# Sequence DFT table built by GpSimd, batch 1's second pc copy by ScalarE, and lower score prices in the order model

## The chip, the cores and the metric

The kernel runs on one core of one Trainium2 chip. The metric is the device time of one execution in microseconds. A profiled execution also has a span, from its first to its last instruction, which is shorter than its device time.

## What is computed

Inputs are q, k and v of 8 batches, 12 heads, 448 positions and 64 channels, and two weights, w1 (768 x 3072) and w2 (3072 x 768). The reference, cut to what matters:

```python
scores = q @ k.transpose(0, 1, 3, 2) / sqrt(64)
attn   = maximum(scores, 0) ** 2 / 448
x      = (attn @ v), heads side by side            # 8 x 448 x 768
mixed  = real(fft(fft(x, axis=1), axis=2))         # over positions, then channels
u      = x + mixed
un     = (u - mean(u)) / sqrt(var(u) + 1e-6)       # over the 768 channels
out    = u + maximum(un @ w1, 0) @ w2
```

The two transforms are done as matrix products with tables of cosines and sines: a channel table (`chan`, and `chan_neg` with the sign of one half turned) and a sequence table (`seq` with cosines and sines, and `nseq`, the sines with the sign turned).

## The kernel before, in words

**Stages of a batch.** Attention works on 21 items a batch (7 for each group of 4 heads). An item is a pair of score products on TensorE (`score`, L939), a Relu of 128 x 896 by ScalarE (`squares`, L952), a square by VectorE (`square`, L969), and then products with v (`value`, L807 and L812), 24 steps in batch 0. Each of the six finished blocks of 128 channels is copied out of PSUM as `xT` (`leave` in `fold`, L656 and L658 for batch 0, L674 for batch 1) and folded by symmetry (L733 for batch 0). The channel transform multiplies the folds by `chan` (L1392 in `first_channels` for batch 0, L1417 in `mix` later). Its result `pp` has two halves of rows. Each is copied from PSUM to `pc` (L1436). Then the sequence transform multiplies `pc` by `seq` and `nseq` (L1014 in `first_tail` for batch 0, L1229 in `mix_rows` for batch 1), u is formed and normalised, and turned for the two big products (L1905 with w1, L1890 or L1892 for its Relu, L1933 with w2 for the first group of 384 rows).

**Start.** GpSimd issues the loads of q, k, v and the weights in one hand-written order (`loading`): the three groups of batch 0, two groups of batch 1's q and k, six half blocks of w1, the rest of batch 1's k, the other half of w1, batch 1's v, then w2 in four quarters, the fourth issued by the second L511 of its pair. Between the first loads it writes index rows (`dft_indices`: four iotas). From these VectorE makes the angles of the tables (`build_dft`): for each piece a product rounded to integer (L328), the fraction (L330) and its absolute value (L332). ScalarE takes sines (L337). The order in `build_dft` is the sequence table first, then the three channel tables; `negative` makes `nseq` from `seq` on VectorE (L374) and `chan_neg` (L378). The first q and k are turned by TensorE against an identity (L608) and copied by VectorE and ScalarE (L615). After batch 0's last Relu, `root_table` (L384) has ScalarE load the table for square roots, which `first_tail` needs.

**Order of the work.** Every engine runs its queue in order. The order is fixed when the program is built, by the class `Streams`: each piece of work is a step of a generator that names its engine, a price in microseconds, the times before which it can't start, and buffers. `Streams` takes again and again the step that can start first by its own clock, and among equals the one of lowest rank. So a price in `need(...)` does not change an instruction's duration on the chip, but changes where it stands in its queue. The prices of TensorE are multiples of `mm(n)`, `n / 2400 + 0.002` us in this stage, of ScalarE `act(n)`, `n / 1200 + 0.17`, from which its clock takes off `OVERLAP`, 0.12. A score step of batch 0 costs `mm(448) + 0.2` (twice `mm` for one item in seven), a value step the same.

**Batch 1's pc.** `mix` copies the first half of `pp` on ScalarE and the second on VectorE. On VectorE's queue stand also the copies of batch 2's q and k into bf16 (L568), which wait for their loads.

Of the kernel before, what the change touches and what calls it, by code (L numbers as in the profile page):

```python
# [10 lines left out]
FP32 = mybir.dt.float32  # L11
# [166 lines left out]
def kernel(  # L178
# [141 lines left out]
    def build_dft():  # L320
# [14 lines left out]
        def sine(dst, y, n, e, sign=1, bias=zero_t):  # L335
            e = yield need("ACT", act(n), [e + LATENCY["DVE"]])
            nc.scalar.activation(dst, y, AF.Sin, bias=bias, scale=sign * 2.0 * math.pi)  # L337
            dft_ready.t = e + LATENCY["ACT"]

        yield need("DVE", 1.1, [indices_ready])  # L340
        nc.vector.tensor_scalar(row[:, 0:2], row[:, 0:2], 1.0 / S, None, op0=ALU.mult)
        nc.vector.tensor_scalar(row[:, 4:7], row[:, 4:7], 1.0 / D, None, op0=ALU.mult)

        f = work.tile([128, 4 * KH], FP32, name="dfty", tag="uA", bufs=1)
        g = work.tile([128, 4 * KH], FP32, name="dfty", tag="uB", bufs=1)
        for i in range(2):
            e = yield from turns(f[:, i * SX:(i + 1) * SX], g[:, i * SX:(i + 1) * SX], col[:, 0:SX], row[:, i:i + 1], SX, i)
        yield from sine(seq[:, 0, :, :].rearrange("p a s -> p (a s)"), g[:, :2 * SX], 2 * SX, e, -1, halfpi)
        yield from sine(seq[:, 1, :, :].rearrange("p a s -> p (a s)"), f[:, :2 * SX], 2 * SX, e)
        seq_ready.t = dft_ready.t  # L350

        def channel_table(m):
            y = early_hid if m == 2 else work.tile([128, 4 * KH], FP32, name="dfty", tag=("u1A", "u1B")[m], bufs=1)
            e = yield from turns(y[:, 2 * KH:4 * KH], y[:, 0:2 * KH], col2, row[:, 4 + m:5 + m], 2 * KH, m % 2)
            yield from sine(chan[m][:, 0, :], y[:, 0:2 * KH], 2 * KH, e, -1, halfpi)
            yield from sine(chan[m][:, 1, :], y[:, 2 * KH:4 * KH], 2 * KH, e)
            chan_made[m].t = dft_ready.t

        yield from channel_table(0)

        def others():

            for m in (1, 2):
                yield from channel_table(m)
            dft_all.t = dft_ready.t

        sch.add(others(), (0, 0.15))

    chan_made, dft_all = [Cell() for _ in range(3)], Cell()

    def negative():

        e = yield need("DVE", 0.35, [seq_ready])
        nc.vector.tensor_scalar(nseq, seq[:, 1], -1.0, None, op0=ALU.mult)  # L374
        nseq_ready.t = e + LATENCY["DVE"]
# [5 lines left out]
    def root_table():  # L381

        yield need("ACT", 1.5, [dft_all, last_relu])
        nc.scalar.activation(drow[:, 7:8], zero_t, AF.Sqrt, bias=eps_t)  # L384
# [56 lines left out]
    def load_group(i, which=(0, 1, 2), parts=(0, 1)):  # L441
# [3 lines left out]
        for x, src in enumerate((q, k, v)):  # L445
# [19 lines left out]
            if i == 0 and x == 1:  # L465
                e = yield need("POOL", 0.95)
# [50 lines left out]
    def loading():  # L517
# [5 lines left out]
        yield from load_w1(0)  # L523
        yield from load_group(NG, (1,), (1,))
# [876 lines left out]
    def mix(b):  # L1401
# [782 lines left out]
```

## Time and profile before

| | us |
|---|---|
| median of 3 runs | 570.84 (569.85 to 572.52) |
| the profiled execution | 572.27 |
| its span | 570.5 |
| busy: TensorE / VectorE / ScalarE / GpSimd | 557.1 / 443.0 / 315.5 / 195.7 |
| TensorE busy in 0 to 10 and 10 to 20 us | 8.09, 8.22 |

The granted TensorE clock is 1.00 throughout. In lines of a timeline the columns are start, busy time, engine, line, operation, output and inputs with their shapes, and count; in brackets stands how long the engine had been idle and what ended that. In a line of waits stand the waiting line, what it waited for, the microseconds in total, how often, and the longest. Consecutive instructions of an engine overlap a little, so the busy time of one can be longer than its distance to the next.

### The profile page before, as it was taken

The numbers are of one execution on the slowest core, as the hardware profiler recorded it, in microseconds if no ns is written. First come the engines' busy times: TensorE is split into PE (matmuls) and PEld (weight loads), VectorE is DVE, ScalarE is ACT, GpSimd is POOL, SyncE is SP. The second block draws the span as 40 slices with busy tenths as digits, with TensorE's granted clock in tenths as the row PEclk, the third lists the DMA queues.
The fourth block names the chain that finished last, engine by engine and source line by source line (L and its number), as shares of the span: only waits on it lengthen the run. The fifth ranks groups of instructions, "written<-read, shape, count | busy, mean of one in ns | idle before, by whom it ended". The sixth has DMA issues, their size and how long they took to land.

```text
span 570.5 us, 11231 instructions
## 1 busy us (share of the span) xinstructions
PE 557.1 (98%) x4211; PEld 352.0 (62%) x4216; DVE 443.0 (78%) x1028; ACT 315.5 (55%) x526; POOL 195.7 (34%) x279
## 2 busy tenths in 40 slices
PE   7999998999999999999999999999999999999997
PEld 5466555644355555545756766766668688668864
DVE  7977674887788977887998897888899967644762
ACT  5967771576655677676786647718615154005400
POOL 8856223614335233463455536325006000000000
PEclk9999999999999999999999999999999999999999
DMA  9999999979977998899899989947415430332012
GB/s 104 184 210 230 182 216 160 241 129 121 185 94 207 206 152 157 135 205 193 178 128 207 203 132 199 170 122 165 111 56 164 118 98 17 83 108 74 1 55 84
DMA packets 152546, 82.44 MB, mean 145 GB/s; under 512 B 118060, under 2 KB 147756, under 8 KB 152492
## 3 DMA queue, kind: packets, MB, share of 16 engines
q0 software_dynamic: 57056, 33.63, 43.8%
q1 hardware_dynamic: 95436, 48.09, 38.0%
q8 instruction: 33, 0.54, 0.4%
q14 instruction: 21, 0.17, 0.1%
HBM read 62.91 MB, written 26.25 MB: 156 GB/s over the span
## 4 chain that ended last, share of the span: by engine, by line
PE 83%; DMA 9%; DVE 4%; POOL 2%; ACT 1%; issue 1%; SPq 0%; DVEq 0%; POOLq 0%; ACTq 0%
PE psF L1905 23%; PE psF L2045 21%; PE psS L1737 8%; PE psS L939 6%; DMA qn<-in_q_dram 6%; PE psS L2045 5%; PE psF L1960 4%; PE psF L812 4%; PE psF L1933 3%; PE psF L1737 2%; PE psS L1417 2%; DVE sq L969 1%; DMA qk<-in_k_dram 1%; DMA kn<-in_k_dram 1%; PE psF L807 1%
## 5 line engine op out<-in xcount | busy, mean ns | idle before, releaser
L1905 PE MATMUL psF<-unT,w 128*128 128x256 bf16 (+2 forms) x1147 | 165.0, 299 | 1.3 <-DVE hT L1890 0.9
L952 ACT ACTIVATE sq<-psS 128x896 bf16<-128x896 f32 x168 | 144.0, 921 | 32.2 <-PE psS L939 31.8
L1905 PEld LDWEIGHTS <-w 128*128 128x128 bf16 x1152 | 110.8, 98 | 50.9 <-issue 6.7
L969 DVE TENSOR_TENSOR sq<-sq 128x896 bf16<-128x896 bf16 x143 | 89.1, 637 | 9.8 <-ACT sq L952 8.9
L2045 PEld LDWEIGHTS <-hT 128*128 128x128 bf16 x648 | 62.5, 98 | 43.6 <-issue 3.9
L1892 ACT ACTIVATE hT<-psF 128x512 bf16<-128x512 f32 (+2 forms) x118 | 58.0, 507 | 42.6 <-PE psF L1905 41.9
L2045 PE MATMUL psF<-w,hT 128*128 128x384 bf16 x336 | 60.1, 326 | 0.7 <-DVE o L1601 0.6
L1601 DVE TENSOR_TENSOR o<-psF,o 128x384 f32<-128x384 f32 x77 | 42.5, 551 | 23.0 <-PE psF L2045 19.2
L939 PE MATMUL psS<-qkT 64*128 64x448 bf16 (+1 forms) x336 | 51.6, 354 | 2.5 <-DVE qkT L615 1.2
L1752 ACT COPY copies<-psS 128x256 f32<-128x256 f32 x57 | 19.9, 374 | 53.9 <-PE psS L1737 49.0
L1260 POOL TENSOR_TENSOR u<-tp,xn 112x385 f32<-112x385 f32 (+2 forms) x14 | 14.7, 1048 | 80.9 <-DVE tp L1240 61.4
L674 DVE TENSOR_SCALAR xT<-psF 128x224 bf16<-128x224 f32 x62 | 21.2, 384 | 22.6 <-PE psF L812 22.6
L461 POOL DMA_DIRECT2D qn<-in_q_dram x21 | 15.5, 740 | 58.4 <-DVE qkr L568 52.3
L939 PEld LDWEIGHTS <-qkT 64*128 64x128 bf16 (+1 forms) x336 | 13.6, 94 | 34.8 <-issue 29.5
L812 PE MATMUL psF<-sq,vn 128*64 128x448 bf16 x246 | 32.7, 362 | 0.4 <-DVE sq L969 0.4
L1737 PEld LDWEIGHTS <-w 128*128 128x128 bf16 x288 | 28.2, 98 | 4.7 <-issue 1.1
L436 POOL DMA_DIRECT2D kn<-in_k_dram x42 | 25.7, 624 | 12.6 <-PE psF L812 7.0
L1269 DVE BATCH_NORM_STATS2 stats<-u 112x6 f32<-112x384 f32 (+2 forms) x56 | 28.5, 542 | 1.0 <-POOL u L1260 0.8
L436 POOL DMA_DIRECT2D vn<-in_v_dram x42 | 26.0, 633 | 9.4 <-DMA w<-in_moe_w_ch_dram 8.2
L461 POOL DMA_DIRECT2D vn<-in_v_dram x24 | 18.9, 787 | 26.9 <-PE psS L939 26.8
L1288 ACT ACTIVATE un<-u,small 113x768 bf16<-113x768 f32 (+2 forms) x21 | 20.9, 1024 | 10.9 <-DVE small L1275 8.3
L812 PEld LDWEIGHTS <-vn 128*64 128x64 bf16 x288 | 12.7, 108 | 21.5 <-issue 17.0
(236 smaller groups left out, 956.0 us busy)
## 6 DMA issues: line engine op xcount, KB each, us to landing
out_dram<-o SPq DMA_DIRECT2D x56, 192.0 KB, 2.2
qn<-in_q_dram POOLq DMA_DIRECT2D x21, 224.0 KB, 5.0
vn<-in_v_dram POOLq DMA_DIRECT2D x24, 192.0 KB, 5.5
w<-in_moe_w_ch_dram POOLq DMA_DIRECT2D x12, 384.0 KB, 9.1
w<-in_moe_w_ch_dram POOLq DMA_DIRECT2D x4, 1152.0 KB, 26.0
kn<-in_k_dram POOLq DMA_DIRECT2D x21, 192.0 KB, 6.6
utop<-u SPq DMA_DIRECT2D x12, 336.0 KB, 3.6
o<-utop SPq DMA_DIRECT2D x16, 192.0 KB, 4.3
```

What stands on the lines that cost most here:

```text
L436: nc.gpsimd.dma_start(out=t[par * Dh:(par + 1) * Dh, par::2], in_=at)
L461: nc.gpsimd.dma_start(out=to, in_=src[b, hs, 0:rows].rearrange("h (p j) d -> p h (j d)", j=j))
L812: nc.tensor.matmul(av[h * Dh:(h + 1) * Dh, 0:S], lhsT=vn_home[:, at:at + Dh], rhs=sq[:, h, :], start=start, stop=stop, skip_group_check=True)
L939: nc.tensor.matmul(sc[:, h, 0:S].rearrange("k (c q) -> k c q", c=4), lhsT=flat[ps, k0:k0 + KB], rhs=qT[ps, pair], start=True, stop=True)
L952: nc.scalar.activation(r, sc[:, :, 0:S], AF.Relu)
L969: nc.vector.tensor_tensor(r, r, r, op=ALU.mult)
L1269: nc.vector.bn_stats(stats[:n, hf, :], u[:n, hf * (D // 2):(hf + 1) * (D // 2)])
L1601: nc.vector.tensor_tensor(o, pc[:, 0:DH], o, op=ALU.add)
L1737: nc.tensor.matmul(ps[:, 0:N], lhsT=lhs, rhs=rhs[:, m], start=(start and m == 0), stop=(stop and m == 2), skip_group_check=True)
L1892: nc.scalar.activation(hs, ps, AF.Relu)
L1905: nc.tensor.matmul(ph[:, i * N:(i + 1) * N], lhsT=w1_sb[m][hf][:, (jj + i) * 128:(jj + i + 1) * 128], rhs=unT[:, m, 0:N], start=(m == 0), ...
L2045: nc.tensor.matmul(pc[:, 0:DH], lhsT=lhs[i], rhs=rhs[i], start=(start and i == 0), stop=(i == KP - 1), skip_group_check=True)
```

## The change

Three things are changed.

1. The sequence table leaves `build_dft`. A new step `seq_table` in `loading`, after the first half of w1, writes its two index rows and makes its angles on GpSimd, with a rounding by adding and subtracting 1.5 * 2^23. VectorE then takes the absolute value by masking the sign bit, and ScalarE takes three sines, `nseq` among them, after batch 0's last Relu. `root_table` comes after these. In `build_dft` the angles of all three channel tables follow each other, and their sines are steps of their own.
2. Batch 1's second pc copy is made by ScalarE.
3. The prices of batch 0's score and value steps go from `mm(S) + 0.2` to `mm(S) + 0.1`.

```diff
     def dft_indices():
-        nc.gpsimd.iota(drow[:, 0:2], pattern=[[128, 2]], base=0, channel_multiplier=1,
-                       allow_small_or_imprecise_dtypes=True)
         nc.gpsimd.iota(drow[:, 4:7], pattern=[[128, 3]], base=0, channel_multiplier=1,
                        allow_small_or_imprecise_dtypes=True)
-        nc.gpsimd.iota(dcol[:, 0:SX], pattern=[[1, SX]], base=0, channel_multiplier=0,
-                       allow_small_or_imprecise_dtypes=True)
...
-        for i in range(2):
-            e = yield from turns(f[:, i * SX:(i + 1) * SX], g[:, i * SX:(i + 1) * SX], col[:, 0:SX], row[:, i:i + 1], SX, i)
-        yield from sine(seq[:, 0, :, :].rearrange("p a s -> p (a s)"), g[:, :2 * SX], 2 * SX, e, -1, halfpi)
-        yield from sine(seq[:, 1, :, :].rearrange("p a s -> p (a s)"), f[:, :2 * SX], 2 * SX, e)
-        seq_ready.t = dft_ready.t
...
+        for m in range(3):
+            yield from channel_table(m)
+
+    def seq_table():
+
+        f = work.tile([128, 4 * KH], FP32, name="dfty", tag="uA", bufs=1)
+        g = work.tile([128, 4 * KH], FP32, name="dfty", tag="uB", bufs=1)
+        yield need("POOL", 0.55)
+        nc.gpsimd.iota(drow[:, 0:2], pattern=[[128, 2]], base=0, channel_multiplier=1,
+                       allow_small_or_imprecise_dtypes=True)
+        nc.gpsimd.iota(dcol[:, 0:SX], pattern=[[1, SX]], base=0, channel_multiplier=0,
+                       allow_small_or_imprecise_dtypes=True)
+        yield need("POOL", 0.3)
+        nc.gpsimd.tensor_scalar(drow[:, 0:2], drow[:, 0:2], 1.0 / S, None, op0=ALU.mult)
+        for i in range(2):
+            yield need("POOL", 0.45)
+            nc.gpsimd.tensor_scalar(f[:, i * SX:(i + 1) * SX], dcol[:, 0:SX], drow[:, i:i + 1], None, op0=ALU.mult)
+        f, g = f[:, 0:2 * SX], g[:, 0:2 * SX]
+        yield need("POOL", 0.75)
+        nc.gpsimd.tensor_scalar(g, f, ROUND, -ROUND, op0=ALU.add, op1=ALU.add)
+        e = yield need("POOL", 1.1)
+        nc.gpsimd.tensor_tensor(f, f, g, op=ALU.subtract)
+        sch.add(seq_sines(f, g, e + LATENCY["POOL"]), (0, 0.3))
+
+    def seq_sines(f, g, e):
+
+        e = yield need("DVE", 0.4, [e])
+        nc.vector.tensor_scalar(g.bitcast(mybir.dt.int32), f.bitcast(mybir.dt.int32), 0x7FFFFFFF, None,
+                                op0=ALU.bitwise_and)
+        flat = seq.rearrange("p t a s -> p t (a s)")
+        for dst, y, sign, bias in ((flat[:, 0], g, -1, halfpi), (flat[:, 1], f, 1, zero_t),
+                                   (nseq.rearrange("p a s -> p (a s)"), f, -1, zero_t)):
+            e = yield need("ACT", act(2 * SX), [e + LATENCY["DVE"], last_relu])
+            nc.scalar.activation(dst, y, AF.Sin, bias=bias, scale=sign * 2.0 * math.pi)
+        seq_ready.t = nseq_ready.t = dft_ready.t = e + LATENCY["ACT"]
...
     def negative():
 
-        e = yield need("DVE", 0.35, [seq_ready])
-        nc.vector.tensor_scalar(nseq, seq[:, 1], -1.0, None, op0=ALU.mult)
-        nseq_ready.t = e + LATENCY["DVE"]
         for m in range(3):
...
         yield from load_w1(0)
+        yield from seq_table()
         yield from load_group(NG, (1,), (1,))
...
-            e = yield need("PE", (1 + (r == 3)) * mm(S) + 0.2, turned_for(0, i), [BS])
+            e = yield need("PE", (1 + (r == 3)) * mm(S) + 0.1, turned_for(0, i), [BS])
...
-            e = yield need("PE", mm(S) + 0.2, [sqs[i][1], ready[m // 2][2]], [BF] if i == its[0] else [])
+            e = yield need("PE", mm(S) + 0.1, [sqs[i][1], ready[m // 2][2]], [BF] if i == its[0] else [])
...
-            en, copy = ("ACT", nc.scalar.copy) if n0 == 0 else ("DVE", nc.vector.tensor_copy)
+            en, copy = ("ACT", nc.scalar.copy) if n0 == 0 or b == 1 else ("DVE", nc.vector.tensor_copy)
```

More of the change, by code (lines that the diff above doesn't have):

```diff
@@ L337, in sine @@
             nc.scalar.activation(dst, y, AF.Sin, bias=bias, scale=sign * 2.0 * math.pi)
-            dft_ready.t = e + LATENCY["ACT"]
-        yield need("DVE", 1.1, [indices_ready])
-        nc.vector.tensor_scalar(row[:, 0:2], row[:, 0:2], 1.0 / S, None, op0=ALU.mult)
+            dft_made.t = e + LATENCY["ACT"]
+        yield need("DVE", 0.2, [indices_ready])
         nc.vector.tensor_scalar(row[:, 4:7], row[:, 4:7], 1.0 / D, None, op0=ALU.mult)
-        f = work.tile([128, 4 * KH], FP32, name="dfty", tag="uA", bufs=1)
-        g = work.tile([128, 4 * KH], FP32, name="dfty", tag="uB", bufs=1)
-        for i in range(2):
-            e = yield from turns(f[:, i * SX:(i + 1) * SX], g[:, i * SX:(i + 1) * SX], col[:, 0:SX], row[:, i:i + 1], SX, i)
-        yield from sine(seq[:, 0, :, :].rearrange("p a s -> p (a s)"), g[:, :2 * SX], 2 * SX, e, -1, halfpi)
-        yield from sine(seq[:, 1, :, :].rearrange("p a s -> p (a s)"), f[:, :2 * SX], 2 * SX, e)
-        seq_ready.t = dft_ready.t
         def channel_table(m):
@@ L354, in channel_table, with sines @@
             e = yield from turns(y[:, 2 * KH:4 * KH], y[:, 0:2 * KH], col2, row[:, 4 + m:5 + m], 2 * KH, m % 2)
+            sch.add(sines(m, y, e), (0, 0.15))
+        def sines(m, y, e):
             yield from sine(chan[m][:, 0, :], y[:, 0:2 * KH], 2 * KH, e, -1, halfpi)
             yield from sine(chan[m][:, 1, :], y[:, 2 * KH:4 * KH], 2 * KH, e)
[L357 to L365, printed above, removed]
@@ L371, in negative @@
+    ROUND = 1.5 * 2 ** 23
+    chan_made, dft_made = [Cell() for _ in range(3)], Cell()
     def negative():
[L373 to L375 removed]
         for m in range(3):
```

7 lines of the change are left out of this document (3 added, 4 removed).

## The prediction

> **What bounds the kernel now.** I read the page first, then the waits of TensorE, then a table of windows, and only then single instructions.
>
> ```profile
> span 570.5 us, 11231 instructions
> PE 557.1 (98%) x4211; PEld 352.0 (62%) x4216; DVE 443.0 (78%) x1028; ACT 315.5 (55%) x526; POOL 195.7 (34%) x279
> ```
>
> TensorE is busy for 557.1 of 570.5 us. So a gain can only be idle time of TensorE taken away, or TensorE work that starts earlier. The waits from 50 us on, and the windows around the changed places:
>
> ```profile
> PE psS L1229 <- DVE pc L1436: 1.7, 1, 1.7
> PE psF L1905 <- DVE hT L1890: 0.9, 1, 0.9
> ```
>
> ```profile
> 20.00:31.00 11.00, 10.10 (x72) 3.87 (x69) 11.00 (x30) 10.99 (x16) 7.20 (x14) 1.00 1.12 188
> 31.00:36.00 5.00, 5.00 (x46) 3.47 (x46) 2.75 (x10) 2.55 (x5) 1.36 (x3) 1.00 1.18 204
> ```
>
> The columns of the windows are length, then TensorE, its weight loads, VectorE, ScalarE, GpSimd, each with its count, then clock, DMA share and GB/s. The largest wait after 50 us is batch 1's second pc copy, the very one that moves. In batch 0's attention VectorE (11.00 of 11.00) and ScalarE (10.99) are both full. So that stage is bound by these two, and batch 0's tail follows it. The chain of waits agrees; its pieces there are:
>
> ```profile
> 15.95 2.54 ACT sq L952 x3
> ...
> 21.41 2.01 DVE sq L969 x4
> ...
> 32.82 3.09 PE psS L1392 x30
> ```
>
> **Part one: the second pc copy of batch 1.**
>
> ```profile
> 90.98 1.04 ACT L1436 CAST pc<-psS 128x772 bf16<-128x772 f32 x1 [4.48 <-PE psS L1417]
> ...
> 91.78 2.11 PE L1933 MATMUL psF<-w,hT 128*128 128x384 bf16 x12
> ...
> 93.73 0.33 PE L1229 MATMUL psS<-pc,seqm 128*128 128x385 bf16 x1
> 94.37 0.43 DVE L568 COPY qkr<-qn 112x1024 bf16<-112x1024 bf16 x1 [5.37 <-DMA qn<-in_q_dram]
> ...
> 94.72 1.01 DVE L1436 CAST pc<-psS 97x772 bf16<-97x772 f32 x1
> ...
> 95.78 1.32 PE L1229 MATMUL psS<-pc,seqm 97*128 97x385 bf16 x7 [1.73 <-DVE pc L1436]
> ...
> 96.47 0.49 ACT L1237 ACTIVATE qs<-psS 128x385 f32<-128x385 f32 x1 [4.46 <-PE psS L1229]
> ...
> 96.94 1.30 PE L1933 MATMUL psF<-w,hT 128*128 128x384 bf16 x7
> ```
>
> The copy needs 1.01 us but stands behind L568, which waits 5.37 us for batch 2's q. The reader sees TensorE issue one row matmul at 93.73 and the next at 95.78. Seven rows take 96.94 - 95.78 = 1.16 us, 0.17 each, so the second was due at 93.90: 1.88 us are lost. After the change ScalarE does both copies, the first to about 92.0, the second at the first's 1.04 us to about 93.1. It has nothing else until 96.47. Both are ready before 93.73, so I take the whole **1.9 us** (bounds 0, if another wait stands there, and 1.9). Next late after that is nothing that the rows name: L1933 goes on at once.
>
> **Part two: the sequence table leaves the start.**
>
> ```profile
> 4.41 0.36 DVE L328 TENSOR_SCALAR dftr<-early,drow 128x240 int32<-128x240 f32 x1
> ...
> 6.60 0.41 DVE L332 SCALAR_TENSOR_TENSOR dfty<-dfty 128x240 f32<-128x240 f32 x1
> ...
> 7.04 1.28 ACT L337 ACTIVATE seqm<-dfty,few 128x480 bf16<-128x480 f32 x2 [5.03 <-DVE dfty L332]
> ...
> 8.80 0.28 DVE L374 TENSOR_SCALAR nseq<-seqm 128x480 bf16<-128x480 bf16 x1
> ...
> 9.98 0.65 DVE L615 COPY qkT<-psF 128x960 bf16<-128x960 bf16 x1
> ...
> 11.14 1.12 ACT L337 ACTIVATE chan<-dfty,few 128x386 bf16<-128x386 f32 x2 [0.25 <-DVE dfty L332]
> ...
> 12.17 0.90 ACT L952 ACTIVATE sq<-psS 128x896 bf16<-128x896 f32 x1
> ...
> 12.97 1.11 ACT L337 ACTIVATE chan<-early,few 128x386 bf16<-128x386 f32 x2
> ```
>
> VectorE loses six operations between 4.41 and 7.01 and nseq at 8.80, 2.9 us; ScalarE loses two sines, 1.28. The three channel tables then follow at once, so all their sines should be over near 10.4 instead of 14.0 (12.97 and 1.11 of busy time). The first score does not gain: its q and k copy (9.98) now stands behind all nine table operations and three negations. But once the relus start, at about 12 as before, the pair of sines at 12.97 is no longer between them: 1.0 us of ScalarE, and 0.26 us of idle time at 15.95 (quoted below) goes too. I take **1.3 us** (bounds 0, if group 1's k keeps the pace, and 2.1, if both later pairs of sines and the idle time count).
>
> **Part three: the same table on GpSimd.** What its load queue waits for between 20 and 36 us, and the rows for the prices:
>
> ```profile
> POOL w L500 <- DMA w<-in_moe_w_ch_dram: 5.2, 4, 1.4
> ...
> POOL kn L436 <- DMA w<-in_moe_w_ch_dram: 2.3, 2, 1.3
> ```
>
> ```profile
> 24.19 1.27 POOL L436 DMA_DIRECT2D kn<-in_k_dram  x2
> 40.53 0.99 POOL L1087 TENSOR_SCALAR un<-u,small 128x768 bf16<-128x768 f32 x1
> ...
> 101.65 1.04 POOL L1260 TENSOR_TENSOR u<-tp,xn 128x385 f32<-128x385 f32 x1
> ...
> 105.84 0.55 DVE L1262 TENSOR_TENSOR u<-tp,xn 112x383 f32<-112x383 f32 x1
> ...
> 169.52 1.14 POOL L1262 TENSOR_TENSOR u<-qs,xn 113x383 f32<-113x383 f32 x1
> 169.89 1.19 DVE L1262 TENSOR_TENSOR u<-tp,xn 113x383 f32<-113x383 f32 x1
> ```
>
> By elements, 240 columns of a tensor_scalar cost 0.31 us, 480 cost 0.62, the 480-column subtraction 1.30: four readers of SBUF, 2.54 us, and with the two iotas and the tiny scaling about 3.4. These stand ahead of the kn issue at 24.19. In this stretch GpSimd waits six times, 7.5 us in all, until an earlier weight block has landed, so I count the delay as **0**: the halves of k lie behind six blocks of weights whenever they are issued. If that cover fell away, batch 1's k would come up to 3.4 us later. At the start the loads behind the two iotas that leave are issued a little earlier; that is 0 as well, since the first score waits for VectorE's copy. Nothing that SP issues is moved.
>
> What is not hidden is VectorE. At 169.89 a VectorE operation with two SBUF inputs took 1.19 us against 0.55 at 105.84, and it ended just 0.42 us after the GpSimd operation beside it had ended: it waited for it. Batch 0's squares are such operations, and VectorE is full there. [...]
>
> [...]
>
> Added on VectorE is one absolute value of 480 columns, about **-0.5** from the 0.36 us of L328's 240. It is also a new wait: behind it in VectorE's queue stand the next squares and folds, and behind those TensorE's values. The plan allots GpSimd 3.6 us; the rows give 3.4, but four readers that each wait for a running square (2.01 / 4 = 0.5 us) make 5.4. So VectorE may stand for 0 to 2.0 us; I take **0**, since a low rank lets squares go first.
>
> **Part four: three sines at the end, and the order.**
>
> ```profile
> 15.95 0.92 ACT L952 ACTIVATE sq<-psS 128x896 bf16<-128x896 f32 x1 [0.26 <-PE psS L939]
> ...
> 31.27 1.28 ACT L384 ACT_TABLE_LOAD   x1
> ...
> 33.66 0.46 DVE L733 TENSOR_TENSOR fold<-xT 128x225 bf16<-128x225 bf16 x2
> ...
> 35.28 1.06 ACT L1436 CAST pc<-psS 128x386 bf16<-128x386 f32 x2 [2.42 <-PE psS L1392]
> ```
>
> Three sines at 0.64 us make 1.9, inside the 2.42 us that ScalarE waits for L1392: **0**, with 0.5 us of cover; without that cover they cost up to 1.9.
>
> The order model now charges TensorE 0.1 us less for each of 45 scores and values. By its old prices (mm, act and OVERLAP in the code) TensorE had 18.1 us of them against 16.7 us of relus and was full, so L1392 came behind the last values: 30 of its 36 instructions run from 32.82 on, 3.09 us to 35.91. By the new ones TensorE has 13.6 us, and the first half fits between scores. Only the last channel block of both halves, 8 instructions of 3.09 / 30 = 0.10 us, must follow the last fold, which ends at 33.66 + 0.46 = 34.12. That makes 34.9 at the earliest: a bound of 1.0 us, the other is 0. I take **0.9 us**.
>
> Front: 1.3 - 1.5 - 0.5 + 0.9 = **+0.2 us** earlier. What passes on of it is limited by a transfer:
>
> ```profile
> L511 POOL DMA_DIRECT2D w<-in_moe_w_ch_dram x4: 826/841/856, 53.1 to 59.6; - x4
> ...
> DMA to landing us min/median/max: 17.8/26.0/31.9
> ```
>
> The last quarter of w2 is issued at 59.6 and lands 31.9 us later, at 91.5; the first matmul that needs it (the fourth chain of L1933) runs at 91.78. So only 0.3 us of any front gain gets past, unless the loads move too; they were backlogged, by the 26.0 us that the median took. A front loss has no such limit. Sum: 0.2 + 1.9 = **2.1 us**. The profiled execution took 572.27 us (span 570.5), which becomes 570.2; it lay 1.43 above the median of the runs, so by the median 570.84 becomes **568.7**.
>
> **The rivals.** [...] (2) *The moved copy gains nothing*, because the plan, which now counts the two copies in a row, puts another late instruction ahead of the rows. Only 0.2 is left: 570.6. Against it: no other producer is late at 93.73. (3) *VectorE waits for GpSimd*, slower than before. [...] It decides from the point where the front loses more than 1.9. For it: VectorE has no idle time in 20 to 31. Against it: the rank.
>
> **How the numbers follow.** The forecast, 568.7, has 0.45, its own range 567.5 to 570.0 from the spread of the runs; (1) 0.28, (2) 0.10, (3) 0.17. The range 566.5 to 572.6 leaves out the better edge of (1) and the worse half of (3). A measurement tells 0.5% from no change, 2.85 us here: below 568.0 lie all of (1) and 0.10 of the forecast, 0.38; above 573.7 lies the far part of (3), where the later order suffers as well, 0.11; between them 0.51.
>
> **What would show it.** Right: no wait of L1229 for pc; channel sines over before the first relu; VectorE squares beside GpSimd readers of 0.9 us or more; few L1392 after the last value; the L1933 chain near 91.5. Wrong: an idle VectorE before the absolute value, ScalarE late with batch 0's pc, or the weights of w2 landing earlier with the work; and a new order in later batches whose waits are over 1 us.

## The result, and the profile after

The median after the change is 573.17 us (571.42 to 576.63, 22 runs) against 570.88 (569.46 to 573.24, 22 runs) before: a ratio of 1.0039 [1.0026, 1.0051]. The change makes the kernel 2.3 us slower. The forecast was 568.7 us, 2.1 us faster, with a range up to 572.6.

The profiled execution of after took 573.88 us. It lay 0.71 above its median, that of before 1.43 above its own. So of the 2.29 us between the medians the two traces can show 573.88 - 572.27 = 1.61. Only 571.7 - 570.5 = 1.2 of these lie inside the span. The device time is longer than the span by 1.77 us in before's trace and by 2.18 in after's, and by 2.09 to 2.19 in all 22 executions of after. In after the lines behind the new table are 16 higher, those of the loads 15: L1392, L1014, L1229, L1190 and L1905 of before are L1408, L1030, L1245, L1206 and L1921 here, L436, L461, L608 and L615 are L451, L476, L624 and L631. The page of after:

```profile
span 571.7 us, 11248 instructions
PE 557.5 (98%) x4223; PEld 352.1 (62%) x4228; DVE 439.6 (77%) x1018; ACT 317.3 (56%) x530; POOL 203.0 (36%) x284
```

VectorE is busy 3.4 us less and GpSimd 7.3 us more: the table has moved. TensorE works as much as before (557.5 against 557.1), and the span is 1.2 longer, so TensorE waits more. Its waits from 20 to 130 us, over 1 us:

```profile
PE psS L1206 <- ACT un L1304: 1.5, 1, 1.5
PE psF L828 <- DVE sq L985: 1.3, 1, 1.3
PE psF L1030 <- ACT qkT L631: 1.3, 1, 1.3
```

The wait of batch 1's rows for the second pc, 1.7 in before, is not there any more. Three others have come. Only the second was in before, with 0.4. The two windows of the prediction, after the change:

```profile
20.00:31.00 11.00, 11.00 (x83) 4.56 (x82) 9.91 (x23) 9.65 (x15) 10.64 (x15) 1.00 1.06 181
31.00:36.00 5.00, 3.52 (x43) 2.87 (x42) 3.21 (x11) 3.83 (x7) 5.00 (x9) 1.00 1.06 157
```

VectorE (third busy column) is no longer full in batch 0's attention, 9.91 of 11.00; GpSimd (fifth) is, with 10.64. TensorE now idles 1.48 of the 5 us behind it. The rows of this stage, in order of time:

```profile
24.46 2.94 DVE L985 TENSOR_TENSOR sq<-sq 128x896 bf16<-128x896 bf16 x5
...
25.27 3.00 POOL L366 TENSOR_SCALAR dfty<-early,drow 128x240 f32<-128x240 f32 x2
28.36 2.03 POOL L369 TENSOR_SCALAR dfty<-dfty 128x480 f32<-128x480 f32 x1
28.67 0.99 ACT L968 ACTIVATE sq<-psS 128x896 bf16<-128x896 f32 x1
30.46 1.20 POOL L371 TENSOR_TENSOR dfty<-dfty 128x480 f32<-128x480 f32 x1
31.61 2.47 POOL L451 DMA_DIRECT2D kn<-in_k_dram  x4
31.69 0.41 DVE L377 TENSOR_SCALAR dfty<-dfty 128x480 int32<-128x480 int32 x1 [1.53 <-POOL dfty L371]
32.69 0.38 PE L828 MATMUL psF<-sq,vn 128*64 128x448 bf16 x2 [1.31 <-DVE sq L985]
...
35.44 0.39 PE L624 MATMUL psF<-ident,qn 112*64 112x112 bf16 x8
...
42.25 0.41 PE L624 MATMUL psF<-ident,kn 128*64 128x128 bf16 x8
42.93 0.96 ACT L631 COPY qkT<-psF 128x960 bf16<-128x960 bf16 x1
43.94 0.49 PE L1030 MATMUL psF<-pc,seqm 128*112 128x384 bf16 x2 [1.28 <-ACT qkT L631]
```

GpSimd needs until 31.6 for the table. VectorE stands 1.53 us before the absolute value, TensorE 1.31 before the square behind that. Then comes what no step of the prediction had: TensorE turns batch 1's first q at 35.44, but its first k only at 42.25, in the midst of batch 0's tail. The two share one `psF` buffer. It stays taken from 35.44 until L631 has copied it out at 43.89, and the tail's last rows wait 1.28 us for that. In before q and k were turned together at 36, and the last rows began at 42.47. The first product with w1 runs at 50.78, before at 49.30. At batch 1's pc and behind it:

```profile
92.46 2.03 ACT L1452 CAST pc<-psS 128x772 bf16<-128x772 f32 x2 [4.48 <-PE psS L1433]
...
95.21 1.49 PE L1245 MATMUL psS<-pc,seqm 128*128 128x385 bf16 x8
96.53 1.79 PE L1949 MATMUL psF<-w,hT 128*128 128x384 bf16 x10
...
102.82 0.59 POOL L451 DMA_DIRECT2D kn<-in_k_dram  x1 [1.42 <-DMA kn<-in_k_dram]
103.42 0.93 POOL L1276 TENSOR_TENSOR u<-tp,xn 128x385 f32<-128x385 f32 x1
104.39 0.56 DVE L1285 BATCH_NORM_STATS2 stats<-u 128x6 f32<-128x384 f32 x1 [2.25 <-POOL u L1276]
...
107.96 0.51 PE L1206 MATMUL psS<-ident,un 128*128 128x128 bf16 x6 [1.51 <-ACT un L1304]
...
119.91 2.32 PE L1921 MATMUL psF<-unT,w 128*128 128x512 bf16 x10
```

ScalarE makes both copies in a row, and eight row products run without a gap. At 96.53 TensorE is 0.41 us ahead of before (96.94). But the turned rows of `un`, at 106.69 before, now run at 107.96 after a wait. The chain behind it reads upwards: un needs VectorE's statistics, these need GpSimd's u, and u stands in GpSimd's queue behind an issue of k that waits 1.42 us for an earlier block to land. The 512-wide products begin at 119.91 against 118.63. From there to the end it takes 571.7 - 119.91 = 451.79 us; before 570.5 - 118.63 = 451.87. So what the traces show of the loss is 1.28 us ahead of 120 us and 0.41 us outside the span.

### The profile page after: what moved, and what is told of

The parts are those of the page before. It is cut to its first block, busy times and chain, and to the rows that moved or that the text cites. A ratio compares the mean times of both kernels' runs of the same rounds, so it can differ in the third digit from the quotient of the medians.

```text
span 571.7 us, 11248 instructions
## 1 busy us (share of the span) xinstructions
PE 557.5 (98%) x4223; PEld 352.1 (62%) x4228; DVE 439.6 (77%) x1018; ACT 317.3 (56%) x530; POOL 203.0 (36%) x284
## 4 chain that ended last, share of the span: by engine, by line
PE 81%; POOL 6%; DMA 6%; DVE 3%; ACT 2%; issue 2%; SPq 0%; POOLq 0%; DVEq 0%; ACTq 0%
PE psF L1921 24%; PE psF L2061 21%; PE psS L1753 8%; PE psS L955 6%; DMA kn<-in_k_dram 5%; PE psS L2061 5%; PE psF L1976 4%; PE psF L828 4%; PE psF L1753 2%; PE psS L1433 2%; PE psF L1949 2%; PE psF L823 1%; PE psS L828 1%; POOL qk L476 1%; ACT sq L968 1%
## 5 line engine op out<-in xcount | busy, mean ns | idle before, releaser
L1921 PE MATMUL psF<-unT,w 128*128 128x256 bf16 (+2 forms) x1147 | 165.0, 299 | 1.3 <-DVE hT L1906 0.9
L1921 PEld LDWEIGHTS <-w 128*128 128x128 bf16 x1152 | 110.8, 98 | 51.0 <-issue 6.7
L476 POOL DMA_DIRECT2D qn<-in_q_dram x21 | 15.5, 737 | 57.8 <-DVE qkr L584 52.1
L828 PE MATMUL psF<-sq,vn 128*64 128x448 bf16 x246 | 32.6, 362 | 1.3 <-DVE sq L985 1.3
L451 POOL DMA_DIRECT2D kn<-in_k_dram x42 | 25.7, 623 | 11.8 <-DMA w<-in_moe_w_ch_dram 6.5
L451 POOL DMA_DIRECT2D vn<-in_v_dram x42 | 26.1, 636 | 10.4 <-DMA w<-in_moe_w_ch_dram 8.0
L476 POOL DMA_DIRECT2D vn<-in_v_dram x24 | 19.0, 796 | 27.6 <-PE psS L955 27.4
L1288 ACT ACTIVATE small<-small,few 112x1 f32<-112x1 f32 (+2 forms) x28 | 8.2, 298 | 32.1 <-DVE small L1286 29.0
```

Of the source, the lines that this page charges most:

```text
L451: nc.gpsimd.dma_start(out=t[par * Dh:(par + 1) * Dh, par::2], in_=at)
L476: nc.gpsimd.dma_start(out=to, in_=src[b, hs, 0:rows].rearrange("h (p j) d -> p h (j d)", j=j))
L828: nc.tensor.matmul(av[h * Dh:(h + 1) * Dh, 0:S], lhsT=vn_home[:, at:at + Dh], rhs=sq[:, h, :], start=start, stop=stop, skip_group_check=True)
L1921: nc.tensor.matmul(ph[:, i * N:(i + 1) * N], lhsT=w1_sb[m][hf][:, (jj + i) * 128:(jj + i + 1) * 128], rhs=unT[:, m, 0:N], start=(m == 0), ...
```

## The experiments

Times are medians; ratios are to before in the same session. The sessions differ: before had 570.69 to 570.94 in those of e1 to e4 and e13 to e16, and 572.19 to 572.55 in those of e5 to e12 and of e17 and e18. After itself was run only where before had 570.88 and 570.94. After without a word means the changed kernel.

**Each part alone.** The first four split the change: the pc copy, the prices, both, and the table with the old prices and pc.

```diff
# e1 (and in e3)
-            en, copy = ("ACT", nc.scalar.copy) if n0 == 0 else ("DVE", nc.vector.tensor_copy)
+            en, copy = ("ACT", nc.scalar.copy) if n0 == 0 or b == 1 else ("DVE", nc.vector.tensor_copy)
# e2 (and in e3)
-            e = yield need("PE", (1 + (r == 3)) * mm(S) + 0.2, turned_for(0, i), [BS])
+            e = yield need("PE", (1 + (r == 3)) * mm(S) + 0.1, turned_for(0, i), [BS])
-            e = yield need("PE", mm(S) + 0.2, [sqs[i][1], ready[m // 2][2]], [BF] if i == its[0] else [])
+            e = yield need("PE", mm(S) + 0.1, [sqs[i][1], ready[m // 2][2]], [BF] if i == its[0] else [])
# e4: after with these three lines as in before
```

> The kernel before, with batch 1's second pc copy on ScalarE and nothing else. Theory A (the GpSimd table costs the front of the kernel, the copy by itself is a gain): the wait of the row matmuls for pc, 1.7 us, is gone, batch 1's later steps move up with it, and the time is 1.2 to 2.0 us lower than before (ratio 0.9965 to 0.998). Theory B (whatever the copy gains is given back at batch 1's normalised rows, because GpSimd's part of u stands behind load issues): TensorE waits 1 to 2 us near 106 for un instead, ratio 0.999 to 1.001.

Measured: 571.63, ratio 1.0022 [0.9996, 1.0048]. The wait for pc is gone and a new one stands behind it; TensorE's waits of e1:

```profile
PE psS L1190 <- ACT un L1288: 1.0, 1, 1.0
```

The 512-wide products start at 117.39, 1.24 before those of before (0.29 of it is there at the first w1 product already, 49.01 against 49.30), but the runs show no gain.

> The kernel before, with the score and value prices of batch 0 at +0.1 and nothing else. Theory A: the first half of the first channel products moves between the scores, batch 0's tail starts 0.3 to 1.0 us earlier, ratio 0.998 to 0.9995. Theory B (the lower prices put batch 1's k transposes into batch 0's tail, where they hold a PSUM bank): the last rows of the tail wait about 1.3 us for ScalarE's copy of the transposes and the first w1 product starts 0.5 to 1.5 us later, ratio 1.001 to 1.003.

Measured: 573.75, ratio 1.0035 [1.0009, 1.0061]. Two of TensorE's waits, and three windows of 2 us (TensorE's busy time is the second number, its granted clock stands ahead of the last two):

```profile
PE psF L1014 <- ACT qkT L615: 2.3, 1, 2.3
...
PE psF L1933 <- DMA w<-in_moe_w_ch_dram: 0.6, 1, 0.6
```

```profile
42.00:44.00 2.00, 0.27 (x8) 0.23 (x5) 1.56 (x6) 1.05 (x3) 1.36 (x3) 1.00 1.03 213
44.00:46.00 2.00, 1.48 (x7) 1.05 (x7) 0.00 (x0) 0.47 (x1) 1.82 (x2) 0.54 1.08 273
46.00:48.00 2.00, 2.00 (x23) 1.72 (x22) 0.79 (x3) 0.99 (x2) 0.08 (x1) 0.60 1.05 248
```

So the shorter prices alone, with no table moved, put k's transposes into the tail and cost 2.3 us there. Behind that gap the clock is granted at 0.54 and 0.60 for some 4 us, and the first w1 product runs at 52.77. Here the wait for pc is there with 1.80 us, although the front is late: batch 2's q is copied only at 98.63.

> The kernel before with both small parts, the copy and the prices, and the table left as it was. Theory A (all of the loss is the table's): ratio 0.995 to 0.998, 1.5 to 2.9 us faster than before. Theory B (the order given by the prices is the loss): ratio 1.000 to 1.003.

Measured: 572.39, ratio 1.0032 [1.0009, 1.0055]. The tail's wait is 2.3 here too, but nothing slows behind it: the next two row products take 0.49 us, e2's 0.80, and the mean granted clock of the execution is 0.999, e2's 0.996. So the first w1 product is at 51.40, 1.37 us before e2's. The 512-wide products are at 118.79: 2.1 late in front, 0.16 late there.

> The changed kernel with the second copy back on VectorE and the prices back at +0.2: only the table on GpSimd is left. Theory A: GpSimd again needs about 7.5 us for the table instead of 3.4, VectorE stands 1 to 2 us before the absolute value, batch 1's k comes late, and the ratio is 1.003 to 1.008. Theory B (the table is free, the order of the prices does the harm): ratio 0.997 to 1.001.

Measured: 577.28, ratio 1.0104 [1.0067, 1.0141]. TensorE's largest wait:

```profile
PE psF L828 <- DVE sq L985: 4.3, 2, 3.6
```

With the old prices the values come early and hit the wait of VectorE for GpSimd in full. The tail's wait of 1.3 us stands here as well.

**What a GpSimd operation costs.** e5 is after with a second copy of the four operations on GpSimd, behind the second half of w1, where VectorE reads PSUM.

```diff
         yield from load_w1(1)
+        ...same two products, rounding and subtraction, into another tile
```

> The changed kernel with the same four GpSimd operations once more, on scratch columns (the subtraction takes a tile from itself; the result isn't used), after the second half of w1, where VectorE reads mostly PSUM. [...] Theory B (these forms are simply that slow on GpSimd): the second copy takes 1.5, 1.5, 2.0 and 1.2 again.

The one execution took 576.96 us. The four operations of the second copy:

```profile
37.32 1.81 POOL L545 TENSOR_SCALAR early<-early,drow 128x240 f32<-128x240 f32 x2
39.22 1.83 POOL L546 TENSOR_SCALAR early<-early 128x480 f32<-128x480 f32 x1
41.13 0.99 POOL L547 TENSOR_TENSOR early<-early 128x480 f32<-128x480 f32 x1
```

A product of 240 columns takes 0.9 us here, where VectorE's statistics (0.57 us each) read PSUM, and 1.5 beside the squares; the rounding 1.83 and 2.03. The four together take 4.63 us here and 6.23 there, where the prediction had 2.54: 2.1 us more than that estimate here, and another 1.6 there. In after a square of 20 to 36 us took 0.636 us on the mean, against 0.614 in before (the prediction's 2.01 / 4 = 0.5 is a distance on the chain, not a duration). So where the squares and the table ran beside each other it was GpSimd that took longer, by 0.6 us a product, and VectorE by about 0.02 a square. Why GpSimd took longer there no run shows.

**Batch 1's q held until k is there.** In e6 (pc and prices), e7 (after) and e8 (after, with the prices of the GpSimd steps near the measured ones) the plan lets the transposes of q wait for k.

```diff
-                e1 = yield need("PE", 4 * 0.07, ready[i][x:x + 1], [] if x else [BF],
+                e1 = yield need("PE", 4 * 0.07, ready[i][x:2 if b else x + 1], [] if x else [BF],
```

> The kernel before with the second copy and the lower prices, and the order model asked to start batch 1's transposes of q only when k has landed too, so that they don't take a PSUM bank before batch 0's tail and hold it through it. Theory A (with the lower prices the held bank is the loss): the wait of 2.3 us inside the tail is gone, the first w1 product starts at 48.3 to 49.3 us instead of 51.4, and the ratio falls from 1.0032 to 0.997 to 1.000. Theory B (the prices hurt by something else, the bank is hidden behind other waits): ratio 1.002 or more.

> The changed kernel with the same rule for batch 1's transposes. Theory A (held bank 1.3 us, VectorE's wait for GpSimd and the late table the rest): the wait of the last rows, 1.28 us, is gone, the first w1 product starts near 49.5 instead of 50.8, ratio 1.000 to 1.003 (from 1.0039), and VectorE still stands 1 to 2 us before the absolute value. Theory B (the bank only covers another wait): the start and the ratio stay.

> The one before, with the order model told what the GpSimd steps took in the trace: 0.6 for the scaling, 1.6 for each product, 2.1 for the rounding, 1.2 for the subtraction, 7.65 us in all instead of 3.6. The absolute value then stands behind all squares but the last fold. Theory A (the misprice is the loss): VectorE's wait of 1.5 us and TensorE's of 1.3 shrink below 0.5, the first w1 product starts another 0.3 to 1.0 us earlier. Theory B (the table itself comes too late whatever VectorE does, because ScalarE's three sines and the load of the square root table follow it): VectorE's wait goes, but ScalarE's first pc copy of batch 0 stays near 35.5 us and the time with it.

Measured: 587.89, 587.28 and 588.68; ratios 1.0257 [1.0208, 1.0305], 1.0247 [1.0213, 1.0281] and 1.0278 [1.0247, 1.0308]. The tail's wait is gone in all three, and in e7 the first w1 product runs at 48.53, 2.25 earlier than in after. But the order of all later batches comes out another way and loses some 15 us. In e8 VectorE does not wait for GpSimd any more, but TensorE waits 2.2 us for ScalarE's pc of batch 0, and the first w1 product runs at 50.15. What these runs do show is the limit by w2; e7's waits from 45 to 130 us:

```profile
PE psF L1949 <- DMA w<-in_moe_w_ch_dram: 2.2, 1, 2.2
PE psF L1949 <- DVE xT L690: 1.0, 1, 1.0
```

**The table on VectorE, and pc back.** e9 is after with the angles on VectorE at a low rank (GpSimd writes the index rows only), e11 the same with the old prices and pc, e10 is after with the second pc copy back on VectorE. e12 is before again, for a second trace.

```diff
# e9, e11
-        nc.gpsimd.tensor_scalar(drow[:, 0:2], ...
-        ...
+        sch.add(seq_angles(f, g, e + LATENCY["POOL"]), (0, 0.3))   # the same five operations by nc.vector
# e10
-            en, copy = ("ACT", nc.scalar.copy) if n0 == 0 or b == 1 else ("DVE", nc.vector.tensor_copy)
+            en, copy = ("ACT", nc.scalar.copy) if n0 == 0 else ("DVE", nc.vector.tensor_copy)
```

> After, but the sequence table's angles (scaling, two products, rounding, subtraction) are made by VectorE at a low rank after the first half of w1 is issued; GpSimd only writes the index rows there. Theory A (GpSimd's 7.5 us of operations are the step that failed): VectorE has no wait before the absolute value (after: 1.53 us), its added work is five operations of about 1.7 us, the kn issue goes back to near 25 to 26 us (after: 31.6), L828 waits for a square 0 to 0.5 us (after: 1.31), and the first w1 product runs at 49.3 to 50.3 (after: 50.78): 571 to 572.5. Theory B (the late place of the table and the held PSUM bank lose the time, whoever makes the angles): the wait of the last rows for batch 1's qkT stays at 1.3 us, the first w1 product stays at 50.8 or later, and the time is 573 to 574.5.

Measured: 572.45, ratio 0.9993 [0.9965, 1.0020]. VectorE's wait for GpSimd is gone, L833 (after's L828) waits 0.3 us, k is issued at 24.49, and still the tail's rows wait 1.4 us and the first w1 product runs at 51.0. Theory A fails for the front: without GpSimd's operations the front is as late, and batch 1's k, issued in time, is turned in the tail all the same, at 42.38. The time is theory A's, though, and the ratio is 1.00 with a front as late as after's.

> Before, with the table moved behind the channel tables and its three sines after the last relu, angles on VectorE at a low rank, pc and prices as before. Against the table move by GpSimd (577.28, L828 waiting 4.3 us for squares): theory A (GpSimd's slowness lost it): L828 waits less than 1 us and the time is 570 to 573. Theory B (the move itself is the loss): L828 waits over 3 us all the same and the time is 575 to 578.

Measured: 574.47, ratio 1.0030 [1.0008, 1.0052]: between the two. L833 waits 2.4 us for squares; VectorE's own five operations now stand among them. Here too k is issued in time, at 24.11, and turned in the tail, at 43.86. The wait for pc is there with 1.32 us, although the first w1 product runs only at 52.39.

> After, but batch 1's second pc copy goes back to VectorE. The table move alone had 577.28, with its pc still on VectorE, and after has 573.17: either the shorter prices or the pc copy is worth some 4 us beside the table. Theory A (the prices let the values come later, so TensorE waits less for VectorE's late squares): 573 to 575, with a wait of L828 of 1.3 us as in after and a wait of L1245 for pc of 0 to 1.9 us. Theory B (the copy is worth it): 576 to 578, with a wait of L1245 or of what stands behind it of 2 us or more.

Measured: 572.41, ratio 0.9996 [0.9974, 1.0018], against 1.0039 and 1.0031 of after. The time is below both theories, nearer to A, and the first w1 product runs at 51.27, later still than after's 50.78. No wait for pc came:

```profile
93.94 0.43 DVE L584 COPY qkr<-qn 112x1024 bf16<-112x1024 bf16 x1 [2.95 <-DMA qn<-in_q_dram]
...
94.28 1.03 DVE L1452 CAST pc<-psS 97x772 bf16<-97x772 f32 x1
...
95.72 1.49 PE L1245 MATMUL psS<-pc,seqm 128*128 128x385 bf16 x8
...
100.69 1.25 POOL L451 DMA_DIRECT2D kn<-in_k_dram  x2
...
106.79 0.50 PE L1206 MATMUL psS<-ident,un 128*128 128x128 bf16 x6
```

The reader sees batch 2's q land at about 93.9, as in before (94.37). TensorE is 2 us late, so VectorE has its copy done before the rows need it. GpSimd's last k issue does not wait, and the rows of un run at 106.79, with no wait, 0.10 later than in before.

> The kernel before, unchanged, for a second trace. If the 1.73 us that L1229 waits for the second pc copy is the same in each execution, it shows 1.6 to 1.9 again; if it hangs on when batch 2's q lands (94.37 in the first trace), it is smaller or gone here, and the first matmul of the 512-wide products then runs up to 1.9 us earlier than 118.63.

The wait for pc in before's second trace:

```profile
96.23 0.99 PE L1229 MATMUL psS<-pc,seqm 97*128 97x385 bf16 x5 [1.51 <-DVE pc L1436]
```

It is 1.51 us, with the 512-wide products at 118.86; the execution took 572.17 us.

**u away from GpSimd's queue.** e13 (after), e14 (the pc part alone) and e15 (before) have VectorE make batch 1's second u rows as well; e16 is after again in the same session.

```diff
-            eng, en, d = ((nc.vector, "DVE", 2 * dve(KN)), (nc.gpsimd, "POOL", 1.8))[i]
+            eng, en, d = ((nc.vector, "DVE", 2 * dve(KN)), (nc.gpsimd, "POOL", 1.8))[0 if b == 1 else i]
```

> After, but batch 1's second u rows (four operations that GpSimd makes at 103.4 to 106.8) are made by VectorE. Theory A (u stands in GpSimd's queue behind load issues that wait for landed blocks, and that is where the pc copy's gain went): the wait of L1206 for un (1.51 us in after) is under 0.5 us, L1206 runs at 106.4 to 107 instead of 107.96, and the time is about 1 us less than after's in the same session, 571.5 to 573 where after has 573. Theory B (un is late for another reason, the copy on ScalarE delaying ScalarE's own queue): the wait of un stays at 1 us or more, with VectorE done early, and the time is after's.

> Before, with only the second pc copy on ScalarE and batch 1's second u rows on VectorE. Theory A: with pc's wait (1.73 us) gone and no wait of un (0.98 in the pc part alone), the 512-wide products start at 116.2 to 116.8 (117.39 in the pc part alone, 118.63 in before), and the time is 1.0 to 2.0 us under before: ratio 0.9965 to 0.9985. Theory B (the gain is given back again at a later load or wait): a new wait of 1 us or more between 107 and 125, or the wait for w2's last quarter at L1933, and a ratio of 0.9985 to 1.002.

> Before, with only batch 1's second u rows on VectorE. In before un does not make TensorE wait, because the pc wait of 1.73 us lies ahead of it. Both theories: the pc wait stays at 1.3 to 1.9 us and the ratio is 0.999 to 1.001; if u by VectorE costs VectorE's later work (the copies of batch 2's q and k stand behind it), up to 1.003.

> After, unchanged, in one session with the other three: ratio 1.0025 to 1.005 as before. If its wait of L1206 for un is smaller in this execution than 1.51 us, the wait hangs on when a block of k lands, and not on the order alone.

Measured: 590.41, 585.29, 584.36 and 572.54; ratios 1.0340 [1.0313, 1.0367], 1.0242 [1.0215, 1.0269], 1.0246 [1.0220, 1.0273] and 1.0031 [1.0015, 1.0047]. In the first three the later batches come out in another order, as with the gate. That is the same loss in e15, which has nothing else of the change; so the forecast for its ratio failed. Between 150 and 200 us TensorE, full in before (49.90 of 50), now reads:

```profile
150.00:200.00 50.00, 44.66 (x284) 23.21 (x283) 41.79 (x93) 30.86 (x45) 23.98 (x32) 0.99 1.01 163
```

So their times say nothing of u, but their traces up to 120 us do. In e13 the rows of un run without a wait, though its front is as late as after's:

```profile
105.77 0.50 PE L1206 MATMUL psS<-ident,un 128*128 128x128 bf16 x6
```

That is 2.2 us earlier than in after, and the 512-wide products start at 118.46 (e14: 116.79). Theory A holds there: the late un was u behind the loads. In e16's trace un waits 1.42 us, and GpSimd's k issue ahead of u 1.81. Also, VectorE does not wait for GpSimd in e16 and L828 waits 0.2 instead of 1.31, and yet the first w1 product runs at 50.42: with the tail's wait behind it, that wait is worth at most 50.78 - 50.42 = 0.36 us.

The other forecast for e15 failed too, and that says more. Its pc is on VectorE as in before, and still no wait for pc is there:

```profile
92.86 0.43 DVE L568 COPY qkr<-qn 112x1024 bf16<-112x1024 bf16 x1 [3.54 <-DMA qn<-in_q_dram]
...
94.04 1.56 PE L1229 MATMUL psS<-pc,seqm 128*128 128x385 bf16 x8
```

Batch 2's q is copied at 92.86, and not at 94.37 and 94.82 as in before's two traces. Against e15, e14 has only the pc copy moved: its 512-wide products start 0.30 us earlier, but its front was 0.60 us earlier already (the first w1 product at 49.00 against 49.60). So this pair shows no gain of the copy.

**Only k's transposes put back.** e17 is after with the plan's time for the landing of batch 1's first k set 4 us earlier. In TensorE's and ScalarE's queues only its eight transposes and the copy of q and k move; in GpSimd's a load of batch 2's v comes to stand ahead of u. e18 is the same with pc's second copy on VectorE.

```diff
-            ready[i][x].t = max(arrived[i, x]) + (1.5 if i % NG else 0.0, 3.0, 6.0, 8.0)[min(i // NG, 3)]
+            ready[i][x].t = max(arrived[i, x]) + (-1.0 if i == NG and x == 1 else (1.5 if i % NG else 0.0, 3.0, 6.0, 8.0)[min(i // NG, 3)])
```

> After, but the plan takes batch 1's first k as landed 4 us earlier than it did, so that its transposes stand beside q's, ahead of batch 0's tail, as in before. Nothing else of the order changes (the first 8 transposes of k and the copy after them). Both theories: the wait of L1030 for qkT (1.28 us) is gone, and the first w1 product runs at 49.0 to 49.8 instead of 50.8 and 50.4; if k lands after 36 us, TensorE waits for it there instead, up to 1.3 us. Theory A (from 92 us on the landing loads set the time): the front's gain is lost in a longer wait of L1206 for un (1.4 and 1.5 us in after, then 2 to 3) or a wait for w2's last quarter, the 512-wide products start at 119 to 120 as in after, and the ratio is 1.002 to 1.004. Theory B (the late front is the loss): they start at 118.0 to 118.8, and the ratio is 0.998 to 1.0015.

Measured: 571.53 against 572.55 of before, ratio 0.9978 [0.9946, 1.0011], where after had 1.0039 and 1.0031.

```profile
31.70 0.41 DVE L377 TENSOR_SCALAR dfty<-dfty 128x480 int32<-128x480 int32 x1 [1.53 <-POOL dfty L371]
...
32.69 0.38 PE L828 MATMUL psF<-sq,vn 128*64 128x448 bf16 x2 [1.31 <-DVE sq L985]
...
35.66 0.39 PE L624 MATMUL psF<-ident,kn 128*64 128x128 bf16 x8
...
42.17 0.49 PE L1030 MATMUL psF<-pc,seqm 128*112 128x384 bf16 x2
...
49.32 0.98 PE L1921 MATMUL psF<-unT,w 128*128 128x384 bf16 x5
...
101.95 0.77 POOL L476 DMA_DIRECT2D vn<-in_v_dram  x1 [1.95 <-DMA kn<-in_k_dram]
...
107.27 0.51 PE L1206 MATMUL psS<-ident,un 128*128 128x128 bf16 x6 [1.80 <-ACT un L1304]
```

The two waits behind GpSimd are there to the hundredth as in after. K's transposes stand elsewhere, with no wait for their load, and the first w1 product is at 49.32, before's 49.30. So the place of these eight transposes was the loss of the front. The ratio is theory B's, or just under it, but after was not run beside it, in the session where before has 572.55, and e9 and e10 had ratios of 1.00 with the front as late as after's; that the late front is also the loss of the whole kernel is therefore not shown. The trace has theory A's start of the 512-wide products, 119.21, and a longer wait of un, 1.80 us, behind the load of v that this edit moved ahead of u; this execution (572.61) lay 1.08 above its median.

> The same with batch 1's second pc copy back on VectorE (after with it there had a ratio of 0.9996 and no wait for pc, with its front 1.9 us late). Theory A (the landing of batch 2's q sets it): with the front on time the wait of L1245 for pc is back with 1.0 to 1.9 us, the 512-wide products start at 118.3 to 118.9, and the ratio is 0.999 to 1.001. Theory B: no wait for pc comes back, they start at 116.6 to 117.4, and the ratio is 0.996 to 0.998, faster than both kernels.

Measured: 571.17, ratio 0.9983 [0.9949, 1.0016].

```profile
89.80 0.72 POOL L476 DMA_DIRECT2D qn<-in_q_dram  x1 [6.77 <-DMA w<-in_moe_w_ch_dram]
...
91.76 0.43 DVE L584 COPY qkr<-qn 112x1024 bf16<-112x1024 bf16 x1 [2.12 <-DMA qn<-in_q_dram]
...
94.36 1.49 PE L1245 MATMUL psS<-pc,seqm 128*128 128x385 bf16 x8
...
105.44 0.50 PE L1206 MATMUL psS<-ident,un 128*128 128x128 bf16 x6
```

No wait for pc came back although the front is on time: in this execution batch 2's q was issued at 89.80, as soon as w2's blocks had landed, and not at 91.74, and it landed 2.6 us earlier than in before. Neither wait at pc nor at un is a property of the order alone; each hangs on a landing. The 512-wide products start at 117.38. e17 and e18 have the lowest ratios of the changed kernels, 1.0 and 1.4 us under before by the medians, but their intervals reach over 1, so that they are faster is not shown. Between the two the place of the copy makes 0.36 us in favour of VectorE, all of it outside the span: the median span is 569.4 in both.

The traces side by side (the last column is the span less the column before it):

| kernel | rows wait for pc | last k issue waits | rows wait for un | 512-wide from | rest |
|---|---|---|---|---|---|
| before | 1.73 | 0 | 0 | 118.63 | 451.9 |
| e12, before again | 1.51 | 0 | 0 | 118.86 | 451.5 |
| e1, pc alone | 0 | 0.61 | 0.98 | 117.39 | 451.9 |
| e3, pc and prices | 0 | 0.42 | 0 | 118.79 | 451.4 |
| after | 0 | 1.42 | 1.51 | 119.91 | 451.8 |
| e16, after again | 0 | 1.81 | 1.42 | 119.45 | 451.3 |
| e9, after, angles on VectorE | 0 | 0 | 0.68 | 119.11 | 451.9 |
| e10, after, pc back | 0 | 0 | 0 | 118.51 | 451.5 |
| e17, after, k early | 0 | 0 (v: 1.95) | 1.80 | 119.21 | 451.3 |
| e18, the same, pc back | 0 | 0 | 0 | 117.38 | 451.3 |

## Why the prediction was wrong

**Two steps failed**, each by about 1.7 us of the 4.4 us between the forecast (2.1 faster) and the result (2.3 slower).

*The front, +0.2 us.* Parts two and four took everything that starts earlier as a gain: "the first half fits between scores", "I take 0.9 us". What they had wrong is what the plan puts in the place that comes free. L1408 does end 0.4 us earlier. But TensorE now reaches batch 1's q ahead of the tail at a time when the plan does not have its k yet. So q takes a `psF` buffer and keeps it, and the tail's last rows find none. Measured: the first w1 product runs 1.48 us later, all of it ended by moving eight transposes (e17).

It is not GpSimd's table that made k late. By the clock of `Streams` itself, when the two kernels are built, k may be turned from 37.44 us on in before and from 37.04 in after. What moved is the turn of q, from 36.98 to 33.19 (34.90 with the prices alone, 35.34 with the table alone). The traces agree: in e2, e9 and e11 k is issued by 24.5 us, as in before, and is turned in the tail all the same. So "I count the delay as 0" in part three held: k's issue moved from 24.19 to 31.61, and nothing waited for its landing (e17 turns k at 35.66 without a wait).

*Part one, 1.9 us.* The wait goes, as forecast (rows at 95.21 in one piece). But between the first w1 product, 1.48 late, and the 512-wide products, 1.28 late, only 0.20 us is won. "Next late after that is nothing that the rows name" was wrong: u is, behind load issues that wait for landings; TensorE waits 1.0 us for it in e1, 1.5 in after. And the 1.9 us stood in the one execution that was read, which lay 1.43 above its median. Of eight traces with pc on VectorE four have the wait (before 1.73, e12 1.51, e2 1.80, e11 1.32) and four have none (e4, e10, e15, e18); it hangs on when batch 2's q lands. Where two kernels of one session differ by the copy alone, e14 and e15, e17 and e18, it gains nothing. Whether before's faster executions have the wait was not seen: both its traces took over 572 us. Rival (2) gave "the moved copy gains nothing" for another late instruction, which is half of it. The chance of 0.10 was too small.

The other terms:

- *Part two, 1.3 us.* The last relu ends at 29.66 instead of 31.25, 1.6 earlier. The size was right, but in part by another way: the first relu starts at 11.18 instead of 12.17, where "The first score does not gain" had ruled that out.
- *Part three, the sizes.* The four readers and the index rows take 7.6 us, not 3.4 (products 1.5 against 0.31, rounding 2.03 against 0.62, subtraction 1.20 against 1.30): the estimate by elements from L1087 was wrong. The -1.5 us for VectorE in the front's sum is a term that no run shows: in after the 13 squares of 20 to 36 us took 0.636 us on the mean against 0.614 in before, 0.3 us in all, and the longest 0.81, so the squares of 0.9 us did not come either. VectorE's wait for GpSimd, "0 to 2.0, I take 0", was 1.53: rival (3)'s mechanism, but it is worth at most 0.36 us at the first w1 product (e16 against after). With the old prices it is the larger part of the loss, 4.3 us of TensorE's waits (e4).
- *Part four, the sines.* Three sines and the square roots' table end at 35.6 on ScalarE, and TensorE waits 0.3 us for ScalarE's pc: the cover of 0.5 was used up.
- *The landing of w2.* No front gain was left for it to limit in after. In e7, with its front 0.8 ahead of before, the wait was there with 2.2 us; but e2, 3.5 late in front, has 0.6 of it too, so this landing moves as well.

What stays open: of 2.29 us the two traces show 1.61. Of these 0.41 lie outside the span. E9, e15, e16 and e17 have that too (medians 2.13 to 2.20 us over the span), e1, e3, e10 and e18 do not (1.75 to 1.80), so it is neither the copy nor the table alone, and its cause is not known. After was not run in the sessions where before has 572.2 to 572.6; a rival that no run excludes is that before itself pays the wait for pc there, and that after would have no loss there either. And why the last k issue waits in some traces (e1, e3, after, e16) and not in others, e9 with pc on ScalarE among them: what delays that landing was not tried.

## What to carry to other kernels

An earlier step is not a pure gain where a plan fills the place that comes free: before pricing it, look for the step that the plan will put there, for what that step still lacks by the plan's clock, and for the buffer that it holds meanwhile. A wait behind a landing (pc behind q, un behind u behind k) is no sum to be won: here it came and went from one trace to the next with the same place in the queue, and when it was removed another landing stood behind it; take it from several traces, and ask whether the median execution has it. And when a small change of a hand-priced order costs ten times its size, the later stages have been reordered: compare only the stretch ahead of that.

## What the runs showed of the hardware that was not expected

GpSimd's tensor_scalars took more than the estimate by elements, 0.31 and 0.62 us: 240 columns took 0.9 us beside VectorE's reads of PSUM (e5) and 1.5 beside its squares (0.99 in e4, with two squares beside two products), 480 columns with two operations 1.83 and 2.03, while the two-input subtraction of 480 took 0.99 and 1.20.

A lower granted clock followed some gaps of TensorE of about 2 us and not others, and in these traces the length of the gap does not tell which. In e2 a wait of 2.26 us (TensorE busy 0.27 of 2 us) was followed by a granted clock of 0.54 and 0.60 until 48 us; in e3, behind a wait of 2.29 us at the same place, the next two row products took 0.49 us, where e2's took 0.80. In e5, behind a wait of 1.77 us, the six products that turn un at 45.31 took 0.85 us and the sixteen at 47.35 1.68; in e13, behind one of 1.72, the same products took 0.50 and 1.06. The clock fell in e4 too, to 0.72 and 0.50 in the 4 us behind its wait of 3.6. What decides between e2 and e3 was not tried.
